# A new order of all steps, and more buffers, in a fused RWKV-5 and squared-ReLU kernel

## The chip, the core and the metric

The kernel runs on one core of one Trainium2 chip. The metric is the device time of one launch in microseconds. Engines are named as in the profile: PE (TensorE) with PEld (its weight loads), DVE (VectorE), ACT (ScalarE), POOL (GpSimd) and SP (SyncE, which here only issues transfers).

## The reference

```python
def _attn_ref(r, k, v, w, u):            # r, k, v: (4, 8, 768, 48); w, u: (8, 48)
    state = zeros((B, H, D, D))
    for t in range(S):
        kt, vt, rt = k[:, :, t], v[:, :, t], r[:, :, t]
        cur = einsum('bhd,bhe->bhde', u[None] * kt, vt)
        y[:, :, t] = einsum('bhd,bhde->bhe', rt, state + cur)
        state = w[None, :, :, None] * state + einsum('bhd,bhe->bhde', kt, vt)

def _moe_ref(x, w_in, w_out):            # x: (3072, 384); w_in: (384, 2048); w_out: (2048, 384)
    h = maximum(x @ w_in, 0.0)
    return h * h @ w_out
```

The output y of the first part, laid out as 3072 tokens of 384 values, is the x of the second.

## The kernel before

**Units and chunks.** A batch's 768 steps are cut into 6 chunks of 128; a unit i is one chunk (i // 4) of one batch (i % 4), all 8 heads, so there are 24 units. Within a unit the recurrence becomes matmuls; between units of one batch a state S0W is handed on.

**Steps.** Each function of the class Do issues one step, for one unit. `ld` loads r, k or v (192 KB in float32). `kh` and `rh` scale k and r by powers of w into the tile rk (the first four units read the powers from PSUM, where `Wk` and `Wt` put them; `WkS` and `WtS` write copies in SBUF for the others). rk is transposed into rkT: by PE (`T`) and a copy (`Tc`), or by a DMA transpose (`XB`). `A` multiplies k and r per head (8 matmuls of 48 rows), `Bm` masks the result, `Y` sums it with v (bf16, made by `vb`) and, from the second chunk on, with the state. `P0`, `P1`, `du`, `dv` make the term with u (r times k, times u, summed per head, times v); `xs` adds it to Y. `U`, `ts`, `S` (or `S0`) carry the state on. xs is transposed into x by PE (`X`) and a copy (`xTc`), or by a DMA transpose (`xX`).

**The second part.** It runs over 13 groups of units (GROUPS: two of one unit, eleven of two). `F1` g.s multiplies x of group g with w_in into a PSUM bank of 512 columns, `re` applies the ReLU into hr, `sq` squares into hq (form 0 on ACT, 1 and 2 on DVE). `F2` i.q adds the matmuls of one quarter q of w_out for unit i; after the four quarters `os` copies the bank out and `out` stores 192 KB.

**Weights.** w_in is cut into eight tiles W1[s]. Seven are loaded in float32 on SP (`lW.0.s`, into the staging tiles wsa) and cast (`cW.0.s`). W1[2] and the four quarters of w_out are loaded by POOL with a cast on the way (`W.0.2`, `W.1.q`). An F1 of a one-unit group needs two W1 tiles (F1.g.2 needs W1[4] and W1[5], F1.g.1 needs W1[2] and W1[3]), one of a two-unit group one.

**The order.** A planner has written all 961 steps into the text ORDER. An entry such as `sq.4.1:A0/26` gives the step, its engine (A is ACT, D DVE, G POOL, P PE, S SP) with a form, and the buffer numbers. The kernel only walks the list (the loop at the end) and each engine runs its own entries in that order; what waits for what follows from the tiles. POOLS gives the number of buffers of each kind. `Z.n.b` is no work: n blocks of 128 columns of matmuls on the identity into bank b, to fill PE's time at the start.

Lines that the profile names: L319 ld, L323 lW, L332 W, L335 kh, L338 rh, L341 P0, L345 P1, L348 du, L353 dv, L362 T, L368 XB, L375 A, L383 Bm, L391 and L393 Y, L402 U, L410 xs, L423 S, L428 X, L435 xX, L444 F1, L452 and L454 re, L459 to L463 sq, L471 F2, L480 Z, L493 out; L259 and L261 are the helper for copies and casts (Tc, xTc, vb, cW, os) on ACT and on the other engines.

Of the kernel before, what the change touches and what calls it, by code (L numbers as in the profile page):

```python
# [30 lines left out]
re.0.2:D/4 xTc.3:A WLm:G U.3:P/1 F1.2.1:P/0 re.1.2:A/5 W.1.2:G sq.0.3:A0/1 F1.2.5:P/1 re.2.1:D/2 W.1.3:G sq.0.0:A0/2
U.1:P/2 S0.2:D re.2.5:A/3 F1.2.4:P/0 sq.0.2:D2/3 cW.0.3:A S0.0:D F1.2.7:P/1 re.2.4:D/1 sq.1.0:A0/4 F2.0.0:P/1
sq.2.5:D2/5 re.2.7:A/4 S0.3:D F1.0.1:P/0 F1.2.3:P/1 re.0.1:D/0 F2.1.0:P/0 S0.1:D re.2.3:A/3 F1.1.1:P/0 sq.1.2:D2/6
sq.0.1:D2/7 ld.k.7:S/6 F1.2.0:P/1 re.1.1:A/5 F2.0.1:P re.2.0:A/0 sq.1.1:D2/8 F1.2.2:P/0 sq.2.4:A0/9 sq.2.0:D1/10
F2.1.1:P kh.4:D/4 F1.2.6:P/1 ld.v.5:S/4 rh.4:D P0.4:D/4 F2.1.2:P ld.r.7:S/6 re.2.2:D/5 P1.4:G F2.0.2:P re.2.6:D/1
sq.2.2:A0/11 F2.1.3:P ld.v.4:S/5 kh.5:G/5 sq.2.1:A0/12 sq.2.6:D1/13 F2.0.3:P os.1:A/0 du.4:D/4 ld.k.6:S/0 T.4:P/0
sq.2.3:A0/14 rh.5:D F2.2.0:P/0 os.0:A/1 P0.5:D/0 Tc.4:A/4 ld.r.6:S/0 T.5:P/3 P1.5:D F2.2.1:P kh.7:D/6 Tc.5:A/5
ld.v.7:S/6 A.4:P/1/2 du.5:D/0 F2.3.0:P/1 Bm.4.0:D/3 ld.k.9:S/2 A.5:P/0/3 vb.4:A/4 dv.4:G Bm.4.1:D/2 F2.3.1:P vb.5:A/5
ld.r.9:S/2 Bm.5.1:D/4 dv.5:G sq.2.7:A0/15 Y.4:P/1 Bm.5.0:D/5 F2.3.2:P rh.7:G ld.k.8:S/1 xs.4:D/4 U.4:P/2 Y.5:P/3
F2.2.2:P P0.6:G/1 ld.v.6:S/0 xs.5:D/0 X.4:P/0 ts.4:D/0 X.5:P/1 T.7:P/3 xTc.4:A/1 kh.6:D/1 ld.k.15:S/3 F2.2.3:P xTc.5:A  # L40
rh.6:D vb.7:A/6 U.5:P/2 P1.6:D F1.3.0:P/0 Tc.7:A/6 ld.k.10:S/4 ts.5:D/1 F1.3.1:P/1 kh.9:D/2 re.3.0:A/0 ld.v.9:S/2
T.6:P/0 P0.7:D/2 os.2:A/2 A.7:P/1/2 S.5:D re.3.1:A/5 ld.r.8:S/1 F2.3.3:P du.6:D/2 P1.7:G Tc.6:A/0 Bm.7.1:D/0 F1.3.3:P/0
sq.3.0:A0/16 rh.9:G ld.r.10:S/3 os.3:D/3 F1.3.4:P/1 re.3.3:A/2 Bm.7.0:D/1 A.6:P/3/0 P0.9:G/3 du.7:D/1 re.3.4:A/1
XB.9:S/1 F1.3.5:P/0 Bm.6.1:D/3 sq.3.1:A0/17 dv.7:G F1.3.6:P/1 Bm.6.0:D/2 re.3.5:A/3 F2.5.0:P/0 dv.6:G vb.6:A/7
ld.k.12:S/5 sq.3.3:A0/18 Y.7:P/2 out.3:S kh.10:D/3 re.3.6:A/4 Y.6:P/1 ld.v.8:S/3 S.4:G xs.7:D/1 F1.3.2:P/0 sq.3.5:A0/19
xs.6:D/2 F1.3.7:P/1 ld.v.11:S/1 kh.8:D/0 re.3.2:A/0 kh.15:D/4 U.6:P/0 X.6:P/3 sq.3.2:A0/20 X.7:P/2 rh.8:D F2.4.0:P/1
ld.r.12:S/4 re.3.7:A/5 rh.10:D F2.5.1:P xTc.6:A/2 sq.3.4:D2/21 P1.9:D xTc.7:A U.7:P/1 T.8:P/3 vb.9:A/2 out.0:S P0.8:D/4
F1.4.0:P/0 ts.6:D/1 ld.k.11:S/0 Tc.8:A/2 P1.8:G ts.7:D/0 F1.4.4:P/1 ld.r.13:S/5 du.9:D/3 re.4.0:A/2 F2.5.2:P kh.12:G/5
re.4.4:A/3 F1.4.6:P/0 ld.r.11:S/0 sq.3.6:A0/23 sq.3.7:D2/22 vb.8:G/3 du.8:D/4 A.9:P/2/0 sq.4.4:A0/24 A.8:P/1/3 S.6:G
re.4.6:A/0 F2.5.3:P ld.v.10:S/5 Bm.8.1:D/4 F1.4.3:P/1 dv.8:G Bm.8.0:D/5 os.5:A/3 ld.k.13:S/6 F1.4.5:P/0 Bm.9.1:D/1  # L50
re.4.3:A/1 dv.9:G Y.8:P/3 Bm.9.0:D/0 re.4.5:A/5 XB.10:S/3 F2.4.1:P P0.12:G/0 xs.8:D/3 sq.4.0:A0/25 Y.9:P/1 vb.11:A/1
kh.11:G/1 F1.4.1:P/1 xs.9:D/4 ld.v.13:S/4 X.8:P/0 F1.4.2:P/0 re.4.1:D/4 xTc.8:A/0 ld.r.15:S/6 F2.4.2:P rh.11:D
sq.4.1:A0/26 P1.12:D X.9:P/2 vb.10:A/0 F1.4.7:P/1 P0.10:D/1 ld.k.20:S/2 xTc.9:A sq.4.5:D2/27 F2.7.0:P/0 P0.11:D/2
re.4.7:A/3 ld.v.12:S/6 U.8:P/3 P1.10:D sq.4.3:A0/28 F2.4.3:P kh.13:D/6 re.4.2:A/2 F1.5.2:P/1 du.10:D/0 out.1:S os.4:A/1
# [63 lines left out]
def kernel(  # L118
# [13 lines left out]
    B, H, S, D = r.shape  # L132
# [410 lines left out]
```

## Time and profile before

| what | us |
|---|---|
| median of 3 runs | 176.91 (175.41 to 177.27) |
| the profiled run's own time | 175.4 |
| span of the profiled run | 173.7 |
| PE, PEld busy | 165.4, 121.9 |
| DVE, ACT, POOL busy | 140.7, 109.8, 69.3 |
| granted TensorE clock | 1.00 throughout |
| DMA | 28.34 MB, 163 GB/s mean |

The times of steps come from one profiled run. A span is counted from the program's first instruction to its last; the run's own time also has what lies around it. Matmuls are pipelined: the time from one start to the next tells what one costs, its length does not. Busy lengths of DVE and ACT overlap by some 0.1 us from one instruction to the next.

### The profile page before, as it was taken

How to read it: one execution, taken by the hardware profiler on the slowest of the kernel's cores; microseconds unless marked ns; L12 is line 12 of the kernel's file. 1: busy time of each engine (PE TensorE's matmuls, PEld its weight loads, DVE VectorE, ACT ScalarE, POOL GpSimd, SP SyncE). 2: the span in 40 equal slices, each digit the busy share in tenths (PEclk: the TensorE clock that was granted, in tenths of full speed). 3: DMA queues.
4: the chain of work that ended last, by engine and by line, in shares of the span. 5: the costliest groups of instructions: out<-in, count | busy, mean ns of one | idle time of the engine just before them, and what ended most of it. 6: DMA issues, size and time to landing. Idle time of an engine off the chain costs nothing.

```text
span 173.7 us, 4402 instructions
## 1 busy us (share of the span) xinstructions
PE 165.4 (95%) x1714; PEld 121.9 (70%) x1714; DVE 140.7 (81%) x278; ACT 109.8 (63%) x203; POOL 69.3 (40%) x84
## 2 busy tenths in 40 slices
PE   4989699999999999999999999999999999999991
PEld 1445498766878787877777787778678677787760
DVE  5989787799899989999989898899998667853520
ACT  2489389557599979786676769659478141173401
POOL 4264743044385694923464950601950301000000
PEclk9999999999999999999999999999999999999999
DMA  5999999999999999989698799989931422110041
GB/s 106 245 249 248 258 213 219 201 192 189 213 188 214 243 171 234 197 191 205 128 217 178 151 205 212 152 191 180 200 94 30 151 94 68 25 45 4 0 171 55
DMA packets 102276, 28.34 MB, mean 163 GB/s; under 512 B 94824, under 2 KB 102256, under 8 KB 102256
## 3 DMA queue, kind: packets, MB, share of 16 engines
q1 hardware_dynamic: 100360, 26.10, 71.4%
q0 software_dynamic: 1744, 1.77, 6.2%
q8 instruction: 13, 0.21, 0.5%
q10 hardware_dynamic: 152, 0.20, 0.3%
q14 instruction: 7, 0.06, 0.1%
HBM read 20.46 MB, written 4.72 MB: 145 GB/s over the span
## 4 chain that ended last, share of the span: by engine, by line
PE 80%; DMA 8%; SPq 6%; ACT 1%; issue 1%; POOL 1%; POOLq 0%
PE bank L471 36%; PE bank L444 33%; DMA wsa<-in_moe_w_in_dram 8%; SPq L319 5%; PE bank L375 3%; PE bank L393 2%; PE bank L391 2%; PE bank L402 2%; PE bank L362 2%; SPq L323 1%; PE bank L428 1%; ACT W L259 1%; ACT hr L452 0%; ACT hq L459 0%; ACT os L259 0%
## 5 line engine op out<-in xcount | busy, mean ns | idle before, releaser
L444 PE MATMUL bank<-xT,W 128*128 128x256 bf16 (+1 forms) x624 | 74.5, 264 | 1.3 <-ACT W L259 1.2
L471 PE MATMUL bank<-W,hq 128*128 128x384 bf16 x384 | 73.6, 326 | 0.0
L452 ACT ACTIVATE hr<-bank 128x512 bf16<-128x512 f32 x71 | 42.0, 597 | 35.9 <-PE bank L444 33.2
L444 PEld LDWEIGHTS <-W 128*128 128x128 bf16 x624 | 55.4, 98 | 11.9 <-ACT W L259 1.4
L471 PEld LDWEIGHTS <-hq 128*128 128x128 bf16 x384 | 35.6, 98 | 17.8
L459 ACT ACTIVATE hq<-hr 128x512 bf16<-128x512 bf16 x57 | 34.7, 629 | 2.5 <-DVE hr L454 2.4
L383 DVE TENSOR_TENSOR Bm<-bank,maskJT 128x512 bf16<-128x512 f32 x48 | 31.4, 683 | 3.0 <-PE bank L375 3.0
L345 POOL TENSOR_TENSOR P<-P,ub 128x384 f32<-128x384 f32 x14 | 15.5, 1110 | 30.0 <-DVE P L341 26.8
L353 POOL TENSOR_TENSOR dv<-ldv,du 128x384 f32<-128x384 f32 x19 | 16.4, 874 | 25.7 <-DVE du L348 21.0
L454 DVE TENSOR_SCALAR hr<-bank 128x512 bf16<-128x512 f32 x25 | 17.1, 689 | 10.4 <-PE bank L444 6.5
L463 DVE TENSOR_TENSOR hq<-hr 128x512 bf16<-128x512 bf16 x35 | 15.0, 457 | 1.9 <-ACT hr L452 1.9
L410 DVE TENSOR_TENSOR xs<-bank,dv 128x384 bf16<-128x384 f32 x24 | 13.2, 553 | 3.5 <-PE bank L393 2.8
L259 ACT COPY os<-bank 128x384 f32<-128x384 f32 x18 | 8.6, 477 | 8.8 <-PE bank L471 8.1
L480 PE MATMUL bank<-identity 128*128 128x512 bf16 (+1 forms) x40 | 11.6, 427 | 2.3 <-POOL identity masks.py:199 2.3
L348 DVE TENSOR_REDUCE du<-P 128x8 f32<-128x384 f32 x24 | 12.9, 543 | 0.0
L341 POOL TENSOR_TENSOR P<-ldr,ldk 128x384 f32<-128x384 f32 x11 | 11.3, 1026 | 3.9 <-DMA ldr<-in_r_dram 3.9
L259 ACT COPY rkT<-bank 128x1024 bf16<-128x1024 bf16 x10 | 10.1, 1015 | 2.9 <-PE bank L362 2.2
L423 POOL TENSOR_TENSOR S0W<-ts,WLm 128x384 bf16<-128x384 f32 x7 | 7.4, 1061 | 10.0 <-PE bank L471 6.7
L393 PE MATMUL bank<-vb,Bm 128*128 128x48 bf16 x192 | 10.8, 183 | 0.3 <-ACT vb L259 0.3
L393 PEld LDWEIGHTS <-Bm 128*128 128x128 bf16 x192 | 9.5, 96 | 1.3 <-issue 0.4
L259 ACT CAST vb<-ldv 128x384 bf16<-128x384 f32 x19 | 9.6, 511 | 0.2 <-DMA ldv<-in_v_dram 0.2
L259 ACT COPY xT<-bank 128x384 bf16<-128x384 bf16 x14 | 6.5, 477 | 5.0 <-PE bank L428 5.0
(61 smaller groups left out, 161.7 us busy)
## 6 DMA issues: line engine op xcount, KB each, us to landing
ldr<-in_r_dram SPq DMA_DIRECT2D x24, 192.0 KB, 3.9
ldk<-in_k_dram SPq DMA_DIRECT2D x24, 192.0 KB, 3.8
ldv<-in_v_dram SPq DMA_DIRECT2D x24, 192.0 KB, 4.0
out_dram<-os SPq DMA_DIRECT2D x23, 192.0 KB, 2.2
wsa<-in_moe_w_in_dram SPq DMA_DIRECT2D x7, 384.0 KB, 5.6
W<-in_moe_w_out_dram POOLq DMA_DIRECT2D x4, 384.0 KB, 7.9
rkT<-rk SPq DMA_TRANSPOSE x14, 3.4
W<-in_moe_w_in_dram POOLq DMA_DIRECT2D x1, 192.0 KB, 8.2
```

Of the source, the lines that this page charges most:

```text
L259: e.copy(o, a)
L345: e.tensor_mul(t, t, ub)
L353: e.tensor_mul(dvb[slot[f"dv{i}"]], loaded("v", i), t)
L383: e.tensor_mul(Bmb[slot[f"Bm{i}{h}"]], heads(bank(f"bA{i}{h}"), 128), mask_b)
L393: e.matmul(y[:, hc, D * h : D * (h + 1)], m[h][:, hc, :], vb[:, 2 * hc + h, :], start=(c == 0), stop=True, skip_group_check=True,)
L410: e.tensor_add(xsb[slot[f"xs{i}"]].rearrange("p (a b) -> p a b", a=HP), heads(bank(f"bY{i}"), 2 * D), dvb[slot[f"dv{i}"]].rearrange("p (a ...
L444: e.matmul(hp[:, fi, :], W1[f // 2][:, c, 128 * (f % 2) : 128 * (f % 2 + 1)], xt[:, c, :], start=(c == 0), stop=(c == CCH - 1), skip_group ...
L452: e.activation(hr, hp, AF.Relu)
L454: e.tensor_scalar_max(hr, hp, 0.0)
L459: e.activation(hq, hr, AF.Square)
L463: e.tensor_mul(hq, hr, hr)
L471: e.matmul(bank(f"bO{i}", "bO")[:, 0:d_model], hqb[slot[f"hq{g},{f // m}"]][:, at : at + L], W2[q][:, f % 4, :], start=(f == 0), stop=(f = ...
```

## The change

Two counts in POOLS are raised, F2 no longer fixes which quarter of w_out comes first, and ORDER is replaced as a whole: the same kinds of steps, 961 of them as before, in another sequence and partly on other engines. The planner that wrote it now has the fetching of instructions in its model of the queues, and tends to put the A steps of two units next to each other.

```diff
-POOLS = dict(ldr=7, ldk=7, ldv=7, ws=0, wsa=4, rk=7, P0=5, dv=5, vb=8, rkT=7, bank=4, bankH=2, bankO=2, Bm=6, xs=5, xT1=2, xT2=3, xT4=1, hr=6, hq=30, os=4, ts=2)
+POOLS = dict(ldr=8, ldk=8, ldv=8, ws=0, wsa=6, rk=7, P0=5, dv=5, vb=8, rkT=7, bank=4, bankH=2, bankO=2, Bm=6, xs=5, xT1=2, xT2=3, xT4=1, hr=6, hq=30, os=4, ts=2)
 ORDER = """
-ld.r.1:S/0 w:A ld.k.1:S/0 u:S Z.48.5:P tab:A ld.k.0:S/1 ld.k.2:S/2 shw:D ld.r.0:S/1 logw:A ld.r.2:S/2 Wt:A/0 P0.1:D/0
-shu:D Wk:A/1 lW.0.6:S/0 rh.1:D/0 kh.1:D ld.v.1:S/0 ld.k.3:S/3 T.1:P/0 kh.0:D/1 Z.16.5:P P1.1:G Tc.1:A/0 kh.2:D/2 rh.0:D
-ld.v.3:S/1 WtS:A rh.2:D P0.2:G/1 A.1:P/1/2 WkS:A T.0:P/3 lW.0.1:S/1 Z.16.5:P P1.2:D ld.r.3:S/3 Tc.0:A/1 du.1:D/0
-P0.0:D/2 cW.0.6:A ld.v.0:S/2 A.0:P/0/3 dv.1:G Bm.1.1:D/0 Z.6.5:P du.2:D/1 T.2:P/2 P1.0:G Bm.1.0:D/1 ld.v.2:S/3 Z.22.5:P
-Tc.2:A/2 Bm.0.0:D/2 Bm.0.1:D/3 lW.0.0:S/2 vb.1:A/0 lW.0.5:S/3 kh.3:D/3 Y.1:P/1 cW.0.1:A lW.0.7:S/0 A.2:P/0/2 xs.1:D/0
-Z.4.5:P P0.3:G/3 vb.3:A/1 du.0:D/2 lW.0.4:S/1 X.1:P/3 Z.8.5:P rh.3:D wc:S xTc.1:A/0 Bm.2.0:D/4 vb.0:A/2 T.3:P/1
-ld.k.4:S/4 dv.0:D Y.0:P/3 Z.13.5:P Tc.3:A/3 vb.2:G/3 Bm.2.1:D/5 P1.3:G xs.0:D/1 A.3:P/0/2 X.0:P/1 cW.0.0:A U.0:P/3
-dv.2:G Bm.3.0:D/1 Z.6.7:P xTc.0:A/1 du.3:D/3 lW.0.3:S/2 F1.1.0:P/0 Bm.3.1:D/0 ld.r.4:S/4 F1.0.0:P/1 re.1.0:D/0 W.1.0:G
-W.0.2:G cW.0.7:G Y.2:P/0 Y.3:P/1 re.0.0:A/1 ld.k.5:S/5 xs.2:D/2 cW.0.5:A dv.3:D F1.1.3:P/0 cW.0.4:A X.2:P/2 F1.0.3:P/1
-re.1.3:D/2 ld.r.5:S/5 xTc.2:A/0 W.1.1:G U.2:P/0 xs.3:D/3 F1.0.2:P/0 re.0.3:A/3 sq.1.3:D2/0 WLcol:A X.3:P/2 F1.1.2:P/1
-re.0.2:D/4 xTc.3:A WLm:G U.3:P/1 F1.2.1:P/0 re.1.2:A/5 W.1.2:G sq.0.3:A0/1 F1.2.5:P/1 re.2.1:D/2 W.1.3:G sq.0.0:A0/2
-U.1:P/2 S0.2:D re.2.5:A/3 F1.2.4:P/0 sq.0.2:D2/3 cW.0.3:A S0.0:D F1.2.7:P/1 re.2.4:D/1 sq.1.0:A0/4 F2.0.0:P/1
-sq.2.5:D2/5 re.2.7:A/4 S0.3:D F1.0.1:P/0 F1.2.3:P/1 re.0.1:D/0 F2.1.0:P/0 S0.1:D re.2.3:A/3 F1.1.1:P/0 sq.1.2:D2/6
-sq.0.1:D2/7 ld.k.7:S/6 F1.2.0:P/1 re.1.1:A/5 F2.0.1:P re.2.0:A/0 sq.1.1:D2/8 F1.2.2:P/0 sq.2.4:A0/9 sq.2.0:D1/10
...
+ld.k.2:S/0 ld.r.2:S/0 w:A u:S tab:A ld.k.0:S/1 ld.v.2:S/0 ld.r.1:S/1 P0.2:D/0 ld.r.0:S/2 shw:D shu:D logw:A ld.k.1:S/2
+WtS:A Wk:A/0 vb.2:G/0 ld.r.3:S/3 Wt:A/1 P1.2:G kh.2:D/0 rh.2:D ld.v.1:S/1 Z.63.5:P T.2:P/0 kh.0:D/1 du.2:D/0 Tc.2:A/0
+ld.v.0:S/2 WkS:A kh.1:D/2 P0.1:G/1 Z.17.5:P A.2:P/1/2 lW.0.1:S/0 rh.0:D T.0:P/3 Bm.2.1:D/0 dv.2:G wc:S rh.1:D Tc.0:A/1
+P0.0:G/2 Z.4.5:P T.1:P/0 Bm.2.0:D/1 ld.k.3:S/3 Tc.1:A/2 rh.3:D/3 Y.2:P/2 P1.0:G A.0:P/3/1 lW.0.0:S/1 xs.2:D/0 Bm.0.1:D/2
+lW.0.7:S/2 Z.3.5:P A.1:P/0/2 vb.1:G/1 Bm.1.1:D/3 ld.k.4:S/4 P1.1:G X.2:P/1 xTc.2:A/0 Bm.1.0:D/4 ld.v.3:S/3 vb.0:G/2
+du.0:D/1 Z.11.5:P Y.1:P/2 WLcol:A kh.3:D dv.0:D WLm:G Z.8.5:P T.3:P/1 Bm.0.0:D/5 Tc.3:A/3 P0.3:D/3 lW.0.6:S/3 Z.6.5:P
+Y.0:P/0 du.1:D/2 cW.0.1:A P1.3:G A.3:P/3/1 xs.0:D/1 lW.0.4:S/4 cW.0.0:A dv.1:D Z.3.5:P X.0:P/0 lW.0.5:S/5 cW.0.7:G
+xs.1:D/2 xTc.0:A/0 ld.r.4:S/4 du.3:D/3 Z.10.5:P X.1:P/2 lW.0.3:S/0 F1.0.0:P/0 Bm.3.0:D/0 xTc.1:A/1 ld.k.5:S/5 vb.3:G/3
+F1.1.0:P/1 Bm.3.1:D/1 re.0.0:A/0 W.1.0:G dv.3:D Y.3:P/0 re.1.0:A/1 U.1:P/2 cW.0.6:G U.3:P/3 xs.3:D/3 sq.1.0:A0/0
+kh.4:D/4 Z.4.0:P X.3:P/1 cW.0.4:G F1.1.3:P/0 xTc.3:D F1.0.3:P/1 re.1.3:A/2 cW.0.5:D W.0.2:G ld.r.5:S/5 U.2:P/0
+F1.0.2:P/0 re.0.3:A/3 S0.2:D W.1.1:G sq.0.0:D2/1 F1.1.2:P/1 re.0.2:A/4 rh.4:D W.1.2:G U.0:P/1 F1.2.4:P/0 re.1.2:A/5
+P0.4:G/4 F1.2.1:P/1 re.2.4:A/1 T.4:P/0 sq.2.4:A0/2 P1.4:G re.2.1:D/0 F1.2.5:P/0 Tc.4:A/4 ld.v.4:S/4 S0.0:D F1.2.0:P/1
+W.1.3:G re.2.5:D/1 A.4:P/1/0 sq.2.5:D2/3 F1.2.6:P/0 cW.0.3:D re.2.0:A/1 F2.0.0:P/1 sq.1.3:A0/4 Bm.4.0:D/3 F1.0.1:P/1
+re.2.6:A/2 sq.2.1:D2/5 sq.1.2:D2/6 sq.0.2:A0/7 F2.1.0:P/0 sq.2.0:D2/8 re.0.1:A/0 Bm.4.1:D/4 F1.1.1:P/0 sq.0.1:A0/9
...
+    quarters = {}
...
         def F2(e, i, q):
...
+            done = quarters.setdefault(i, [])
+            done.append(q)
             for f in range(4 * q, 4 * q + 4):
...
-                    start=(f == 0), stop=(f == FCH - 1), skip_group_check=True,
+                    start=(f == 4 * q and len(done) == 1), stop=(f == 4 * q + 3 and len(done) == 4),
+                    skip_group_check=True,
```

Steps by engine where the counts differ, before and after:

| step | before | after |
|---|---|---|
| P0 | D 13, G 11 | D 10, G 14 |
| P1 | D 10, G 14 | D 9, G 15 |
| kh | D 19, G 5 | D 14, G 10 |
| rh | D 18, G 6 | D 8, G 16 |
| dv | D 5, G 19 | D 8, G 16 |
| S | D 9, G 7 | D 2, G 14 |
| vb | A 19, D 2, G 3 | A 10, D 5, G 9 |
| cW | A 6, G 1 | A 2, D 2, G 3 |
| xTc | A 14 | A 10, D 4 |
| sq | A 57, D 39 | A 63, D 33 |
| re | A 71, D 25 | A 70, D 26 |
| os | A 18, D 6 | A 16, D 8 |
| out | S 23, A 1 | S 15, A 9 |
| T with Tc, XB | 10, 14 | 9, 15 (unit 11) |
| X with xTc, xX | 14, 10 | 14, 10 (12 by PE, 19 by DMA) |

Behind the start, A steps of two units follow each other on PE six times before and nine times after. The last steps of the new order are:

```text
os.20:D/1 F1.12.3:P/1 sq.12.0:D2/26 out.20:A os.21:D/0 re.12.7:A/0 F2.23.0:P/0 re.12.3:D/5 out.21:A F2.23.2:P
sq.12.7:D2/11 sq.12.3:D2/20 F2.22.0:P/0 F2.23.1:P F2.23.3:P F2.22.3:P os.23:D/2 F2.22.1:P out.23:A F2.22.2:P os.22:A/3
out.22:S
```

## The prediction

> **What bounds the kernel now.** I read the page's busy shares first, then PE's timeline, the chain of waits and the windows, and last the lines of the engines that get more work.
>
> ```profile
> PE 165.4 (95%) x1714; PEld 121.9 (70%) x1714; DVE 140.7 (81%) x278; ACT 109.8 (63%) x203; POOL 69.3 (40%) x84
> ```
>
> PE is busy 95% of the span, but part of that is the Z steps (L480), matmuls on the identity that only fill time. The timeline of PE (start, length, group; in brackets the idle time and what ended it) shows where they end:
>
> ```profile
> 18.75 0.49 PE L480 MATMUL bank<-identity 128*128 128x512 bf16 x3
> 20.48 1.51 PE L444 MATMUL bank<-xT,W 128*128 128x128 bf16 x24 [1.23 <-ACT W L259]
> ...
> 24.25 0.84 PE L444 MATMUL bank<-xT,W 128*128 128x128 bf16 x12
> ```
>
> The first F1 starts at 20.48 after waiting for ACT's cast of a W1 tile. The chain of waits names what stands behind the cast, the transfer of that tile:
>
> ```profile
> 13.93 5.59 DMA wsa<-in_moe_w_in_dram
> 19.54 0.88 ACT W L259
> ```
>
> After that PE is packed. The windows give PE 10.00 of every 10.00 us, and start-to-start times agree: six 256-column F1 matmuls take 0.66 us and four F2 matmuls 0.65 us all the way from 20.5 to the end of the last one at 170.07, with no gap over 0.25 us. So the time is a start (20.5), 149.6 us of packed PE work, and a tail of 3.6 to the span's end at 173.7 (last copy, store, drains). The profiled run took 175.4; the median of the runs, 176.91, is 1.5 above it. I make the sum against 175.4 and add 1.5.
>
> A plan can win only at the start, or by less PE work; every new wait of PE behind the start is a loss, since nothing there absorbs it.
>
> **PE work, part by part.** One PE transpose of r and k goes (T.11, to a DMA): eight matmuls, 0.44 us (38.26 to 38.70 in the timeline). X and xX are only exchanged (12 for 19): nothing. "A in pairs" is priced by these lines:
>
> ```profile
> 39.80 0.81 PE L471 MATMUL bank<-W,hq 128*128 128x384 bf16 x4
> 40.55 0.40 PE L375 MATMUL bank<-rkT 48*128 48x128 bf16 x8
> 40.88 0.82 PE L471 MATMUL bank<-W,hq 128*128 128x384 bf16 x4
> ...
> 59.50 0.82 PE L444 MATMUL bank<-xT,W 128*128 128x256 bf16 x6
> 60.25 0.62 PE L375 MATMUL bank<-rkT 48*128 48x128 bf16 x16
> 60.80 0.82 PE L471 MATMUL bank<-W,hq 128*128 128x384 bf16 x4
> ```
>
> A lone A takes 0.33 and a pair 0.55, so a pair saves 0.11; and the step before an A lasts 0.75 instead of 0.65, so each entry into A costs another 0.10. Behind the start the old order has six pairs and the new one nine: 3 x 0.21 = 0.6. PE work: -1.0 in all. The new use of start and stop in F2 adds no instruction: nothing.
>
> **The start.** First the arithmetic ahead of F1. In the new order P0.2 stands ahead of both shuffles on DVE, and needs the second load, which lands near 4.64: shw slips from 4.02 to about 5.2, logw on ACT to 5.8, and WtS (0.6) now goes ahead of Wk, so kh.2 starts near 7.5 (kh.1 before: 6.3). From there DVE has 23 instructions up to xs.1: 6 Bm at 0.60 and 17 others at 0.47 (lengths 0.68 and 0.55 less the overlap of neighbours in the timeline), 11.6 us, plus 0.4 of waits for T, Tc and k: 19.5. X.1 follows and F1.0.0 starts at about 20.0, 0.5 earlier than the first F1 now. The W1 tile that is awaited today comes earlier (11 loads and 2 tiles ahead of its end instead of 12 and 2), but DVE takes over as the limit.
>
> More matters five steps later, at F1.0.2, which starts at 24.25 now and in the new order needs tiles 4 and 5. Tile 5 is the sixth W1 tile, behind 13 loads, 5 other tiles and wc. The same bytes were through in the trace when ld.k.4 landed, at 23.57, with the DMA share at 0.94 to 1.10 in every 5 us up to there. Its cast goes to DVE, which shows no cast of this size: half of it takes DVE 449 ns, so 0.9 (ACT 887, POOL 880). That gives 24.5. Tiles land late within a mix (5.6 us median from issue, 8.1 at most), so I take 25.0, with 23.5 (PE's own work, tiles in time) and 26.5 as bounds. By F1.0.2 the new order has done one X and one U more (0.34). The start: +0.75 - 0.34 = +0.4.
>
> **The W2 quarters.** GpSimd issues them and the last W1 tile, in a queue that is now longer:
>
> ```profile
> 18.87 0.89 POOL L332 DMA_DIRECT2D W<-in_moe_w_out_dram  x1
> 19.76 0.76 POOL L332 DMA_DIRECT2D W<-in_moe_w_in_dram  x1
> ...
> 26.15 1.41 POOL L332 DMA_DIRECT2D W<-in_moe_w_out_dram  x2
> ```
>
> and from their issue it takes this long until they land (view of tile W):
>
> ```profile
> DMA to landing us min/median/max: 7.1/8.2/9.1
> ```
>
> In the new queue cW.0.7, cW.0.6 and cW.0.4 (0.88 each, the last not before 23) stand ahead of W.0.2, which is issued at 24.0 instead of 19.76; with the median 8.2 it lands at 32.2. F1.0.1 needs it: from 25.0 come eight F1 and F2 steps (5.3) and U, T and A (1.0), so 31.3. PE waits 0.9. W.1.3, behind P0.4 and P1.4, goes out at 28.8 and lands by 37.9 at the longest; F2.0.3 is due ten steps after F1.0.1, at 32.2 + 6.6 = 38.8: covered by 0.9. Bounds of this part: 0, and 2.6 (W.0.2 out at 24.8 and 9.1 under way).
>
> **Moves between engines.** DVE hands 26 operations to GpSimd (rh 10, S 7, kh 5, P0 3, P1 1); GpSimd also takes 6 vb and 2 cW and gives up 3 dv, 31 more in all. By the rows GpSimd needs 1.00 to 1.11 us for what DVE does in 0.57 to 0.62. DVE takes 14 others (xTc 4, vb 3, dv 3, cW 2, os 2) and was not on the path behind 20.5, so its gain is nothing; ACT swaps vb, xTc and cW for six more sq, nothing either; GpSimd's longer times are hidden as long as its queue keeps up, which is the second rival. Eight stores go from SP's queue to ACT's: SP saves 8 x 0.53, ACT pays the same (0.35 in the one case shown), beside 63% busy: nothing, but each waits for its copy and holds back re and sq behind it; four of them stand in the tail, where PE's last eight quarters (5.2 us) cover them. The last store goes the other way, 1.9 to landing on either queue: nothing. Eight buffers and six tiles add no work; they free SP from waits such as the 1.24 us at 18.3 for a staging tile. Instruction fetches moved 0.21 MB and took 0.5% of the DMA time; planning with them changes places, not work: nothing.
>
> **Sum.** -1.0 + 0.4 + 0.9 = +0.3: 175.7 against the profiled run's 175.4, and 177.2 as a median.
>
> **Rivals.**
>
> *Tiles in time: faster.* If tile 5 lands with the DVE chain, F1.0.2 starts at 23.5, the W2 quarters keep their places, and the sum is -1.0 - 0.75 - 0.34 = -2.1: 174.8. For it: no wait for a staging tile any more. Against: the DMA share is 0.94 to 1.10 in every 5 us from 5 to 25, so the bytes cannot come much sooner.
>
> *GpSimd becomes the bound from about 50 to 100 us: slower.* In the windows (busy us and count of PE, PEld, DVE, ACT, POOL; then clock, DMA share, GB/s) GpSimd has room now:
>
> ```profile
> 60.00:70.00 10.00, 10.00 (x119) 7.56 (x118) 9.10 (x17) 8.36 (x18) 7.77 (x9) 1.00 1.05 206
> 80.00:90.00 10.00, 10.00 (x107) 7.26 (x105) 9.25 (x19) 7.01 (x15) 4.87 (x5) 1.00 0.86 173
> ```
>
> Laying both orders along PE's work with the rows' mean times, GpSimd gets 31 us in these 50 before (measured: 32) and 47 after, 94%. It runs in order and also waits for loads and for DVE; some loads lead their reader by only 3.8 us of PE work (k of 8, 14, 18), about the 3.8 a load takes to land, where the old order gave 5.3. What comes late next is rh or kh, with it XB on SP's queue, the loads behind it, and A; an XB leads its A by at least 4.6 and lands in 3.4, so 1.2 is covered. It decides once its 49 operations there fill the 50 us, at 0.06 more each than the rows' means (one more in five at 1.33 instead of 1.00). Beyond that every wait of GpSimd counts: four short-led loads at 0.5 and as much for du (for which it waits 21.0 us in the trace), 4.0 less the 1.2, about 3 on PE: 180.2. These lines bear on it (min, median, max):
>
> ```profile
> L335 DVE TENSOR_TENSOR rk<-ldk,Wkhat x15: 544/548/1348, 34.5 to 107.2; 128x384 bf16<-128x384 f32 x15
> L338 POOL TENSOR_TENSOR rk<-ldr,Wt x6: 996/1000/1315, 42.9 to 100.3; 128x384 bf16<-128x384 f32 x6
> ```
>
> Both engines have cases far over their median. The Trainium skill (SBUF — State Buffer, "SBUF: two separate sides") says that DVE and GpSimd share a port pair under an exclusive lock, and that a DVE instruction with two SBUF inputs and a GpSimd one block each other fully. The long cases agree with it. Against the rival: fewer such DVE instructions remain, 68 for 101.
>
> *The W2 quarters starve: slower.* With the bound of 2.6 for F1.0.1's wait the sum is +2.0: 178.9. For it: all DMA engines are taken up there; against: the old order's landings are from the same crowded stretch.
>
> **Chances.** Forecast (within its own 176.0 to 178.5) 0.40; tiles in time 0.20; GpSimd 0.29; W2 0.11. A measurement of this kernel can tell about 1%, 1.8 us, from no change. Faster by more than that: the first rival nearly whole, 0.19. Slower: GpSimd's, most of W2's and a little of the forecast's upper end, 0.40. The range runs from the first rival's 174.8 to 181.0, a little over GpSimd's.
>
> **What would show it.** Right: first F1 near 20.0, F1.0.2 near 25.0 after a wait for DVE's cast; PE gap-free from about 33 on; GpSimd over 9 of 10 us between 50 and 100. Wrong: PE waits between 50 and 100 that lead back to GpSimd's rk, S or dv, or an F1.0.2 outside 23.5 to 26.5.

## The result: 3.9% slower, and one store on ACT behind most of it

The changed kernel takes 183.32 us (median; 182.83 to 184.5), the kernel before 176.39 in the same comparison: a ratio of 1.039, 95% interval 1.031 to 1.047. The profiled execution took 184.5 with a span of 182.8, against 175.4 and 173.7 before.

The busy shares come first. PE lost three points, and GpSimd has half as much work again:

```profile
PE 167.8 (92%) x1711; PEld 123.0 (67%) x1711; DVE 140.5 (77%) x261; ACT 104.2 (57%) x188; POOL 102.7 (56%) x115
```

DVE has 17 instructions fewer than before and is busy for the same time (140.7 before). GpSimd has 31 more and 33 us more.

The start, in PE's timeline (start, length, group; in brackets the idle time and what ended it), and DVE's timeline of the same stretch:

```profile
20.40 1.56 PE L446 MATMUL bank<-xT,W 128*128 128x128 bf16 x24
...
23.97 0.38 PE L485 MATMUL bank<-identity 128*128 128x512 bf16 x1 [1.40 <-DVE xs L412]
...
24.35 1.50 PE L446 MATMUL bank<-xT,W 128*128 128x128 bf16 x24
...
25.87 0.33 PE L446 MATMUL bank<-xT,W 128*128 128x128 bf16 x3
```

```profile
21.74 1.49 DVE L355 TENSOR_TENSOR dv<-ldv,du 128x384 f32<-128x384 f32 x1
23.36 0.56 DVE L412 TENSOR_TENSOR xs<-bank,dv 128x384 bf16<-128x384 f32 x1
...
24.83 0.94 DVE L261 CAST W<-wsa 128x768 bf16<-128x768 f32 x1
```

The first F1 starts at 20.40; then PE stands 1.40 us for xs.3, which stands behind a dv.3 of 1.49 us where its kind takes 0.55. F1.0.2 starts at 25.87, 1.62 later than before, just when the cast of tile 5 is through (25.77).

From there PE is nearly packed up to 76, and then comes the one big hole. PE's timeline, then ACT's:

```profile
75.60 0.81 PE L475 MATMUL bank<-W,hq 128*128 128x384 bf16 x4
81.23 1.44 PE L446 MATMUL bank<-xT,W 128*128 128x256 bf16 x6 [4.82 <-ACT hr L454]
```

```profile
73.18 1.25 ACT L454 ACTIVATE hr<-bank 128x512 bf16<-128x512 f32 x2
80.18 0.36 ACTq L498 DMA_DIRECT2D out_dram<-os  x1
80.58 0.60 ACT L454 ACTIVATE hr<-bank 128x512 bf16<-128x512 f32 x1 [6.15 <-DMA ldv<-in_v_dram]
```

PE waits for a re on ACT, since both F1 banks are full. ACT did nothing from 74.44 to 80.18: the store out.3 stood at the head of its queue. The release is named on the third line: the landing of a load of v, which is none of the store's business by its data. In the compiled program the transfers of SP and ACT raise eight completion semaphores in turn, 101 to 108 in the trace. This turn isn't the order of the text ORDER, in which ld.v.15 stands just behind out.3: in the compiled program ld.v.15, on SP's queue, is the eighth transfer ahead of out.3, and both raise semaphore 101. The store waits until ld.v.15 has landed (80.16) and goes out 0.02 us later. Its copy os.3 had been done 21 us before ACT got to the store.

Why was ld.v.15 late? SP's timeline and GpSimd's lead back:

```profile
64.12 1.84 SPq L321 DMA_DIRECT2D ldv<-in_v_dram  x2
71.04 4.23 SPq L370 DMA_TRANSPOSE rkT<-rk  x2
75.33 1.20 SPq L321 DMA_DIRECT2D ldk<-in_k_dram  x2
76.57 1.56 SPq L321 DMA_DIRECT2D ldv<-in_v_dram  x2
```

```profile
57.46 1.93 POOL L355 TENSOR_TENSOR dv<-ldv,du 128x384 f32<-128x384 f32 x2 [3.13 <-DVE du L350]
...
68.75 1.31 POOL L337 TENSOR_TENSOR rk<-ldk,Wkhat 128x384 bf16<-128x384 f32 x1
70.02 0.99 POOL L340 TENSOR_TENSOR rk<-ldr,Wt 128x384 bf16<-128x384 f32 x1
```

SP issued nothing from 65.97 to 71.04. It stood at the transposing transfer XB.11 until GpSimd had finished rh.11, at 71.02. GpSimd had waited 3.13 us for a du of DVE and worked without a gap from then on. Behind XB.11 and XB.10 came two loads of k, and at 76.57 ld.v.15, which landed 3.59 later.

The windows (busy us and count of PE, PEld, DVE, ACT, POOL; then clock, DMA share, GB/s) show the same and one thing more:

```profile
60.00:70.00 10.00, 9.92 (x119) 7.97 (x117) 10.00 (x18) 6.68 (x13) 10.00 (x10) 1.00 0.78 162
70.00:80.00 10.00, 6.41 (x55) 4.69 (x53) 7.84 (x11) 3.53 (x7) 10.00 (x11) 1.00 0.75 127
80.00:90.00 10.00, 8.77 (x81) 6.10 (x81) 4.78 (x9) 6.70 (x13) 7.31 (x8) 0.66 1.07 234
```

GpSimd and DVE are full from 60 to 70, and the granted clock, 1.00 all along before, is 0.66 from 80 to 90. In the trace it is 0.5 from 80.03 to 86.85; PE worked in 5.6 us of that, so this cost 2.8.

The last F2 ends 9.14 us later than before. In the sum a wait of PE is counted from where PE would have gone on without it, 0.1 to 0.2 us more than the idle time in brackets. F1.0.2 gives +1.62, but one X and one U more are done by then (-0.34); the hole gives 4.98, the half clock 2.8, two waits at 30 and 51 give 0.33 and 0.51; PE's own work is -0.8 (worked out below). That is 9.1, for this one execution, the longest of the changed kernel's.

### The profile page after: what moved, and what is told of

Its sections match the earlier page's. It is cut to its first block, busy times and chain, and to the rows that moved or that the text cites. A ratio compares the mean times of both kernels' runs of the same rounds, so it can differ in the third digit from the quotient of the medians.

```text
span 182.8 us, 4369 instructions
## 1 busy us (share of the span) xinstructions
PE 167.8 (92%) x1711; PEld 123.0 (67%) x1711; DVE 140.5 (77%) x261; ACT 104.2 (57%) x188; POOL 102.7 (56%) x115
## 4 chain that ended last, share of the span: by engine, by line
PE 57%; SPq 20%; DMA 8%; POOL 6%; DVE 4%; issue 2%; ACT 1%; ACTq 0%; POOLq 0%
PE bank L475 26%; PE bank L446 24%; SPq L321 16%; SPq L325 3%; PE bank L377 2%; DMA ldk<-in_k_dram 2%; DMA ldv<-in_v_dram 2%; DMA ldr<-in_r_dram 2%; DMA out_dram<-os 2%; PE bank L395 2%; PE bank L393 1%; POOL P L347 1%; DVE Bm L385 1%; POOL rk L337 1%; POOL rk L340 1%
## 5 line engine op out<-in xcount | busy, mean ns | idle before, releaser
L446 PE MATMUL bank<-xT,W 128*128 128x256 bf16 (+1 forms) x624 | 75.5, 267 | 5.1 <-ACT hr L454 4.8
L446 PEld LDWEIGHTS <-W 128*128 128x128 bf16 x624 | 56.6, 99 | 17.1 <-issue 5.8
L461 ACT ACTIVATE hq<-hr 128x512 bf16<-128x512 bf16 x63 | 38.1, 628 | 6.6 <-DVE hr L456 6.1
L340 POOL TENSOR_TENSOR rk<-ldr,Wt 128x384 bf16<-128x384 f32 x16 | 18.7, 1171 | 9.1 <-DMA ldr<-in_r_dram 9.0
L425 POOL TENSOR_TENSOR S0W<-ts,WLm 128x384 bf16<-128x384 f32 x14 | 14.6, 1047 | 12.6 <-DVE ts L422 12.5
L343 POOL TENSOR_TENSOR P<-ldr,ldk 128x384 f32<-128x384 f32 x14 | 14.9, 1072 | 8.4 <-DVE du L350 7.0
L259 ACT COPY rkT<-bank 128x1024 bf16<-128x1024 bf16 x9 | 9.1, 1009 | 7.6 <-PE bank L364 7.5
L259 ACT COPY os<-bank 128x384 f32<-128x384 f32 x16 | 7.6, 476 | 9.6 <-PE bank L475 9.5
L337 POOL TENSOR_TENSOR rk<-ldk,Wkhat 128x384 bf16<-128x384 f32 x10 | 11.2, 1118 | 0.5 <-PE bank L404 0.5
L465 DVE TENSOR_TENSOR hq<-hr 128x512 bf16<-128x512 bf16 x25 | 10.1, 438 | 0.2
```

The costliest lines, as they stand in the source:

```text
L259: e.copy(o, a)
L340: e.tensor_mul(rk[slot[f"rk{i}"]][:, 0, :, 0:D], loaded("r", i), early("WtP") if i < EARLY else Wt2)
L446: e.matmul(hp[:, fi, :], W1[f // 2][:, c, 128 * (f % 2) : 128 * (f % 2 + 1)], xt[:, c, :], start=(c == 0), stop=(c == CCH - 1), skip_group ...
L461: e.activation(hq, hr, AF.Square)
```

## The experiments

Times are medians; each ratio is to the kernel before in the same comparison.

**Is it the store on ACT?** One entry of the new order is changed.

```diff
-out.3:A
+out.3:S
```

> The changed kernel with one entry of the order altered: the store out.3 goes from ACT's queue to SP's. Theory L (the store stands at the head of ACT's queue until the load ld.v.15 of SP's queue has landed, ACT's re copies stand behind it, PE runs out of banks for 5.0 us, and the granted clock then falls to 0.5 for 6.8 us): no wait of PE near 76 us, no stretch at half clock, so 183.3 - 5.0 - 3.4 = 174.9, and some of it given back where the store now stands on SP: 175 to 178. Rival G (GpSimd, busy 10 of 10 us from 60 to 80, is what stalls PE, and the store only shows it first): PE waits within the next 10 us all the same, for rh, XB or A, and the time stays at 180.5 or more.

Measured: 179.25, ratio 1.016 (1.010 to 1.022). The hole at 76 is gone, while GpSimd is as full as it was:

```profile
60.00:70.00 10.00, 10.00 (x120) 8.08 (x119) 9.98 (x19) 7.17 (x14) 10.00 (x10) 1.00 0.94 193
70.00:80.00 10.00, 9.56 (x100) 7.39 (x98) 9.52 (x14) 7.47 (x16) 10.00 (x10) 1.00 0.91 172
```

PE's only wait there is 0.44 us idle for a ts. So rival G, that a full GpSimd stops PE for several us here by itself, falls. Theory L has the place right and the time too low (179.25 lies between the two forecasts), because ACT then stands for another transfer of SP:

```profile
107.59 0.60 ACT L454 ACTIVATE hr<-bank 128x512 bf16<-128x512 f32 x1 [0.32 <-PE bank L446]
111.45 0.48 ACT L259 COPY os<-bank 128x384 f32<-128x384 f32 x1 [3.26 <-DMA out_dram<-os]
```

Here it stands at os.11, whose buffer is still being stored by out.7: a wait for data this time, not for a shared semaphore. That store stood far back in SP's queue: issued at 106.77, 23 us after its copy, landed at 111.43. PE lost 2.3 us and ran at half clock for 3.4.

**The same store, still on ACT, but earlier.** If ACT's queue is the point and not the engine that issues, an earlier place is enough.

```diff
-... xs.9:D/3 os.5:A/0 ... F1.5.2:P/1 out.3:A vb.12:G/2
+... xs.9:D/3 out.3:A os.5:A/0 ... F1.5.2:P/1 vb.12:G/2
```

> The changed kernel with one entry of the order moved: the store out.3 stays in ACT's queue, but ahead of the copy os.5, some 5.5 us earlier. The transfer that raised its completion semaphore before it is then ld.v.11, landed at 67.67 in the changed kernel's trace; ACT comes by at about 68.9. Theory L (only the wait for the late load holds ACT): ACT passes in 0.4 us, no wait of PE near 76, 178 to 180.5 like the run with the store on SP. Rival (a store in ACT's queue in this crowded stretch costs PE several us wherever it stands, as transfers are slow there): 182 or more.

Measured: 178.29, ratio 1.013 (1.009 to 1.018), where the changed kernel had 1.039. The medians differ by 5.0 us, but the kernel before was 0.7 faster in this comparison too; by the ratios a single entry moved within its queue is worth 4.5 us. ACT's timeline and PE's:

```profile
68.50 0.35 ACTq L498 DMA_DIRECT2D out_dram<-os  x1
68.89 0.48 ACT L259 COPY os<-bank 128x384 f32<-128x384 f32 x1 [1.37 <-DMA ldv<-in_v_dram]
```

```profile
71.19 1.47 PE L446 MATMUL bank<-xT,W 128*128 128x256 bf16 x12 [0.30 <-ACT xT L259]
...
75.10 0.82 PE L446 MATMUL bank<-xT,W 128*128 128x256 bf16 x6
75.85 0.45 PE L377 MATMUL bank<-rkT 48*128 48x128 bf16 x9
76.76 0.38 PE L377 MATMUL bank<-rkT 48*128 48x128 bf16 x7 [0.46 <-DVE ts L422]
```

Even here ACT waits 1.37 us at the store for a load of v, another one (ld.v.11), where 0.4 was expected. ACT works without a gap from there to the copy xTc.8, for which PE then stands 0.30 us at 71: a wait of this length is nearly covered. The time is as theory L has it. Together the two runs show the cause of the hole: the wait of a store for a load of another queue, at a place where ACT has no slack for it.

**A store on ACT in the old order**, as a control:

```diff
-out.1:S
+out.1:A
```

> The kernel before with one entry of the order altered: its store out.1, in the middle of the kernel, goes from SP's queue to ACT's. Theory L: what a store on ACT costs is the wait for a load of SP's queue that is late; here SP is on time, the load concerned has landed when ACT gets to the store, so ACT pays its 0.36 us and PE nothing: within 1% of before (175 to 178). Rival (a store in ACT's queue in the middle of the kernel costs PE several us whatever the loads do): 179 or more.

Measured: 175.82, ratio 0.999 (0.995 to 1.004), as theory L says. ACT's timeline:

```profile
67.64 0.60 ACT L452 ACTIVATE hr<-bank 128x512 bf16<-128x512 f32 x1
68.04 0.35 ACTq L493 DMA_DIRECT2D out_dram<-os  x1
68.14 0.62 ACT L459 ACTIVATE hq<-hr 128x512 bf16<-128x512 bf16 x1
```

The load that this store waits for, ld.v.13, landed only at 68.02 in the trace, 0.02 us before the store went out. ACT was still busy with a re then and lost nothing. So a store in ACT's queue in the middle of the kernel costs nothing when SP's load is there in time, and here it was only just in time.

**Does the delay begin with GpSimd?**

```diff
-S.6:G ... ld.r.14:S/0 P1.12:G ... kh.14:G/6 ... rh.11:G
+S.6:G ... ld.r.14:S/0 rh.11:G P1.12:G ... kh.14:G/6 ...
```

> The changed kernel with rh.11 moved ahead of P1.12 in GpSimd's queue, so that it ends some 2.2 us earlier; out.3 stays on ACT. Theory L with its root in GpSimd (rh.11 late, XB.11 at the head of SP's queue late, the loads behind it late, the store on ACT waits for them): SP leaves XB.11 near 68.8 instead of 71.0, ACT's wait and PE's shrink by 1.4 to 2.2 us (the store now stands behind the landing of another load, issued up to 0.9 later), and the clock may stay up: 181.5 at most, 178 if the half clock goes with it. Rival (the store's wait does not begin with GpSimd): no change, 182.5 to 184.

Measured: 183.74, ratio 1.039 (1.030 to 1.047): no gain in the median. The profiled execution, 181.18, is the shortest, and does what theory L says. SP's timeline and PE's:

```profile
67.58 3.12 SPq L370 DMA_TRANSPOSE rkT<-rk  x2
70.75 1.25 SPq L321 DMA_DIRECT2D ldk<-in_k_dram  x2
72.05 2.28 SPq L321 DMA_DIRECT2D ldv<-in_v_dram  x2
```

```profile
78.26 0.92 PE L446 MATMUL bank<-xT,W 128*128 128x256 bf16 x6 [3.08 <-ACT hr L454]
```

XB.11 leaves 3.5 us sooner and PE loses 3.2 us instead of 5.0, with 3.41 us at half clock instead of 6.83. The three other runs had spans of 182.0 to 182.3 at a mean clock of 0.981, which is some 6.9 us at half clock; there is no trace of them, and why they gained nothing stays open. The trace shows the chain from rh.11 to PE; by the median the rival's forecast (182.5 to 184) holds, so what an earlier rh.11 is worth isn't shown.

**The half clock.** A filler Z of 16 matmuls (3.5 us; the expectation took it for four) goes into the hole, the store stays.

```diff
-F1.5.0:P/1
+Z.64.0:P F1.5.0:P/1
```

> The changed kernel with one more filler step Z (four matmuls on the identity, 0.6 us by the rows, to a bank of its own) just ahead of the F1 step that waits near 76 us; the store out.3 stays on ACT. Theory C (the half clock follows PE's idle stretch, some 4 us after it began): idle time falls from 5.0 to about 4.3, the wait ends at the same place; the stretch of half clock is gone or clearly shorter, and the time is 183.3 - 3.4 = about 180 (181.5 if half of the stretch is left). Rival (the half clock has another cause, or 4.3 us of idling are as bad as 5.0): still 6.8 us at 0.5, 182.5 to 184.

```profile
77.74 3.62 PE L485 MATMUL bank<-identity 128*128 128x512 bf16 x16
82.56 0.82 PE L446 MATMUL bank<-xT,W 128*128 128x256 bf16 x6 [1.20 <-ACT hr L454]
```

The clock stays at 1.0 behind the hole, as theory C says, but the time doesn't follow: 183.11, ratio 1.040 (1.034 to 1.047). In this profile a half-clock stretch fell into the start instead, F1 was about 1.5 us later by 52, and behind the hole PE, at full clock, ran into waits of 0.77 (xs, at 89) and 0.40 (sq, at 118). The other runs, at a mean clock of 0.999 to 1.0, took 182.2 to 183.7. So in this order the half clock at 80 was worth little by itself; that its cost would be waited anyway, for engines that are late, is likely from these two waits and not shown.

The reverse: the kernel before without its last three Z steps ahead of F1, which compute nothing that is used.

```diff
-Z.8.5:P ... Z.13.5:P ... Z.6.7:P
```

> The kernel before without its last three steps Z (26 matmuls' worth on the identity that only fill the time between 15.2 and 19.2; nothing the output needs). Theory C (a stretch in which PE idles is followed by 3.4 us, or a multiple of it, at half clock, beginning within 4 us): a stretch at 0.5 between 18 and 25 us, which costs PE up to 1.7 us: 177 to 178.5, clock 0.99. Rival (the half clock in the runs with waits near 76 and 110 came with the load there, and idling alone does not bring it): clock 1.0 throughout, 175.5 to 176.8.

Windows of this run:

```profile
20.00:24.00 4.00, 2.80 (x30) 2.80 (x31) 1.21 (x2) 1.26 (x3) 2.65 (x4) 0.50 1.11 253
24.00:28.00 4.00, 4.00 (x65) 4.00 (x63) 2.67 (x6) 3.50 (x7) 0.38 (x2) 0.71 1.22 245
```

The clock is 0.5 from 19.46 to 26.29. Time 176.98, ratio 1.007 (1.003 to 1.010): between the two forecasts, a hair under theory C's and 0.2 above its rival's. The clock decides for theory C. With the same loads and the same work that the output needs, idling alone brought the half clock here.

**What is left of the loss.** First the second wait, out.7 ahead of out.8 on SP, with out.3 on SP:

```diff
-out.3:A ... out.8:S ... rh.19:G/2 out.7:S
+out.3:S ... out.7:S out.8:S ... rh.19:G/2
```

> The run with out.3 on SP, and out.7 moved ahead of out.8 in SP's queue (it stood at 106.77 there, 23 us after its copy; ACT's os.11, which writes the same buffer, stood until it had landed at 111.43, and PE lost 2.3 us at 110 and 1.7 at half clock). Theory L2 (what is left of the loss behind 70 us is this one wait of the same kind: ACT at the head of its queue for a transfer of SP): no wait of PE over 0.6 us behind 35 us, 175 to 177. Rival (each wait removed is followed by the next, since GpSimd, SP and DVE are all late in this order): again over 1.5 us of PE waits between 70 and 130, 178 to 180.

Measured: 178.55, ratio 1.014 (1.008 to 1.019). The 2.3 us at 110 shrank to 0.39, but the next wait was 1.15 for a Bm at 114. The rival holds, by its time and by the waits: PE's idle stretches between 70 and 130 still add up to 1.7 us. In the profiled execution F1 started only at 21.37, with the start of the program unchanged (20.40 in the changed kernel), so the start differs by 1 us from one execution to another. Then the start as well:

```diff
-P0.2:D/0 ld.r.0:S/2 shw:D shu:D logw:A ld.k.1:S/2 WtS:A Wk:A/0
+shw:D shu:D P0.2:D/0 ld.r.0:S/2 logw:A ld.k.1:S/2 Wk:A/0 WtS:A
...
-Bm.3.0:D/0 ... Bm.3.1:D/1 ... dv.3:D
+dv.3:D Bm.3.0:D/0 ... Bm.3.1:D/1 ...
```

> As the run before, and in the start: both shuffles of w and u ahead of P0.2 on DVE, Wk ahead of WtS on ACT, dv.3 ahead of the two Bm.3 on DVE. Theory S (the start is the chain shuffle, logw, Wk, then DVE's instructions up to xs.1, and a wait for xs.3 behind a dv.3 of 1.4 to 1.5 us): kh.2 starts 0.8 to 1.2 us sooner than 7.58, F1 at 19.2 to 19.5, the wait at 22.4 falls from 1.4 to under 0.8; 1.0 to 1.5 us less than the run before: 174 to 175.8, under the kernel before. Rival (the W1 tiles and their casts are what end the start, as in the kernel before): DVE's chain is earlier, F1.0.2 stays near 25.5, within 0.5 us of the run before.

Measured: 179.22, ratio 1.021 (1.016 to 1.026). kh.2 did start sooner, at 6.33 (7.29 to 7.58 in the other profiles of this start), but DVE then waited 0.45 for Wt on ACT and 0.78 for a load of k. It was nearly packed from there, and xs.1 ended at 20.00, within the 19.9 to 21.2 of the other profiles; F1 started at 20.23 and F1.0.2 at 25.25. The rival holds in its outcome. Its reason, the W1 tiles, isn't what the profile shows: DVE's chain is, and the load that it waits for. A new wait of 1.27 for a ts came up at 51.

**The engines alone.** The old order with the new engines for rh, kh, S, P0, P1 and dv from unit 4 on, and the new order (out.3 earlier on ACT) with the old ones.

```diff
-rh.10:D ... kh.8:D/0 ... S.5:D ... P0.8:D/4
+rh.10:G ... kh.8:G/0 ... S.5:G ... P0.8:G/4
...
```

> The order of the kernel before, with the engines of the change for rh, kh, S, P0, P1 and dv from tile 4 on: 41 of these go from DVE to GpSimd and 18 the other way; stores, loads and PE's order stay. Theory K (the moves are not free: GpSimd fills up, its operations and DVE's two-input ones get in each other's way, and what waits for them is late): over 18 GpSimd operations above 1.2 us where the kernel before has some 13, PE waits of 1 us or more in sum behind 35 us, 177.5 to 182. Rival (the prediction's reading: GpSimd's longer times are hidden): 175 to 176.8.

> The other way round: the changed kernel with out.3 earlier on ACT (178.3 us), and the same operations from tile 5 on back on the engines that the kernel before gave them (40 to DVE, 18 to GpSimd). Theory K: GpSimd's busy time falls from 104 to near 84 us, the long operations of DVE go back from 27 towards 13, the PE waits behind 35 us (0.47 + 0.53 + 0.82 + 0.55 in that run) fall under 1 us: 175.5 to 177.3. Rival (the waits come of the order, which was laid out for these engines; DVE, busy 10 of 10 us from 50 to 70, is then later still): 178 or more.

The moves by themselves: 180.37, ratio 1.020 (1.012 to 1.028), in theory K's range; GpSimd's instructions over 1.2 us went from 7 to 17, where it expected over 18. The only profile of that kernel is of its longest run (183.4, the shortest took 178.97), so what it shows may not hold for the others. In it PE stands 2.0 us at 56 for a Bm, which stands behind a P0 and a dv of DVE at twice their length:

```profile
58.27 0.22 PE L393 MATMUL bank<-vb,Bm 128*128 128x48 bf16 x2 [1.99 <-DVE Bm L383]
```

```profile
54.14 1.24 DVE L341 TENSOR_TENSOR P<-ldr,ldk 128x384 f32<-128x384 f32 x1
...
56.37 1.25 DVE L353 TENSOR_TENSOR dv<-ldv,du 128x384 f32<-128x384 f32 x1
57.54 0.68 DVE L383 TENSOR_TENSOR Bm<-bank,maskJT 128x512 bf16<-128x512 f32 x1
```

The other way round theory K fails and its rival holds: 186.6, ratio 1.058 (1.053 to 1.063). GpSimd's busy time falls to 80.1 and DVE's instructions over 0.7 us stay many (31, against 25), but DVE now has 154.9 us of work and PE waits in some sixteen places behind 35 us, mostly for xs, Bm, xT and hq. So in both of these orders the engines alone could not be exchanged without a loss.

**The parts that lessen PE's work, in the old order.** Two pairs of A and XB.11 in place of T.11; then the pairs alone. The pair of units 6 and 7 is one of the changed order; that of 4 and 5 isn't, and stands for the others.

```diff
-A.4:P/1/2 du.5:D/0 F2.3.0:P/1 Bm.4.0:D/3 ld.k.9:S/2 A.5:P/0/3
+du.5:D/0 F2.3.0:P/1 ld.k.9:S/2 A.4:P/1/2 A.5:P/0/3 Bm.4.0:D/3
...
-A.7:P/1/2 ... Bm.7.1:D/0 ... Bm.7.0:D/1 A.6:P/3/0
+A.7:P/1/2 A.6:P/3/0 Bm.7.1:D/0 Bm.7.0:D/1
...
-T.11:P/2 ... Tc.11:A/4
+XB.11:S/4 ld.k.17:S/1
```

> The kernel before with parts of the change that lessen PE's work, and nothing else: A.4 moved to A.5 and A.7 to A.6 (two more pairs), and T.11 with its copy Tc.11 replaced by a transposing DMA XB.11 ahead of ld.k.17 on SP. Theory W (the prediction's prices: 0.21 for each pair, 0.44 for T.11): 0.86 us less, 174.4 to 175.2 where before is 175.7 to 176.4, no new wait of PE. Rival (XB.11 takes 1.2 to 2.5 us at the head of SP's queue, the loads behind it are late, and a new wait near 75 us takes the gain): 175.7 or more.

> The kernel before with the two pairs alone (A.4 at A.5, A.7 at A.6); T.11 stays on PE. Theory W (a pair saves what the prediction priced, 0.21 each): 0.4 less than before, about 175.6 where before is 176.0. Rival (the A that is moved back comes later, so do its two Bm on DVE and the Y behind them; in the run with XB.11 PE waited 0.40 us for a Bm at 43, and 0.5 at 54): the pairs give nothing or cost up to 0.7: 176.0 to 176.7.

Measured: 177.90, ratio 1.009 (1.005 to 1.013), and for the pairs alone 176.66, ratio 1.003 (1.000 to 1.006). The rival holds both times. PE's timeline from Y.4 to the F2 behind it, first in the kernel before, then with the pairs alone:

```profile
42.62 0.21 PE L391 MATMUL bank<-S0W,rkT 128*128 128x96 bf16 x1
...
43.00 0.81 PE L471 MATMUL bank<-W,hq 128*128 128x384 bf16 x4
```

```profile
42.40 0.21 PE L391 MATMUL bank<-S0W,rkT 128*128 128x96 bf16 x1
...
42.97 0.20 PE L393 MATMUL bank<-vb,Bm 128*128 128x48 bf16 x1 [0.34 <-DVE Bm L383]
...
43.28 0.81 PE L471 MATMUL bank<-W,hq 128*128 128x384 bf16 x4
```

The price of PE's work was right: Y starts 0.22 sooner. But it takes 0.88 instead of 0.38, as PE waits for the Bm behind the A that was moved back. This pair saves 0.2 and costs 0.5. With XB.11 come PE waits for an os (0.71 at 99) and a transposed x (0.59 at 109).

## Why the prediction was wrong, by its steps

**The step that failed** is in "moves between engines": "Eight stores go from SP's queue to ACT's ... nothing, but each waits for its copy and holds back re and sq behind it". The issue on ACT was priced, 0.35 us, and the wait for the copy was named; the other wait, for a transfer of SP's queue that raises the same completion semaphore, was not looked for. In the profiled run that term measured 5.0 us of standing PE and 2.8 of half clock. Taking it away gave 4.1 us (store on SP) and, by the ratios, 4.5 (store earlier): less than 7.8, since other waits came up where the store moved to SP, and since the filler run shows that the half clock added little of its own. The loss of clock was missing from every case of the prediction.

**GpSimd as the bound** was the second rival, 0.29 at 180.2. Its chain was right as far as it went: GpSimd filled all of 60 to 80 (from 50 to 100 it was busy 41 us, not 47), rh was late, XB stood at SP's head, the loads behind it were late. But it was to come out at A, for about 3 us after 1.2 of cover; it came out at ACT, which the chain did not contain. The prediction named PE waits that lead back to GpSimd's rk as a sign of being wrong, and the wait at 76 does lead back to rh.11 in the trace; the median of the run with rh.11 earlier doesn't confirm it. With the store away, the same full GpSimd came with 0.5 us of waiting there. What the prediction did with its other half, "hidden as long as its queue keeps up", was too kind: the moves alone cost the old order 2.0%.

**Price of the moves.** The prediction priced what DVE hands over and takes as nothing, since DVE was not on PE's path. Its busy time is indeed the same, 140.5 against 140.7, but not because nothing changed. With the median lengths of the kernel before, the changed set of DVE's instructions would take some 8 us less (an estimate from the two traces); longer instructions took back 6.7. The lines of the P0 products, before and after (min, median, max):

```profile
L341 DVE TENSOR_TENSOR P<-ldr,ldk x13: 545/551/1285, 4.7 to 115.1; 128x384 f32<-128x384 f32 x13
```

```profile
L343 DVE TENSOR_TENSOR P<-ldr,ldk x10: 546/674/1352, 4.5 to 127.6; 128x384 f32<-128x384 f32 x10
```

The median itself has grown. Over all of DVE, instructions longer than 0.7 us went from 9 to 24, GpSimd's over 1.2 us from 7 to 19. The prediction held against this rival that fewer two-input DVE instructions remain; there were fewer, but more of them were long. The long cases fit the Trainium skill (SBUF — State Buffer, "SBUF: two separate sides"), whose exclusive lock the prediction cited; no run here isolates the lock.

**The start**: first F1 20.0 forecast, 20.40 measured, by the DVE chain as worked out. F1.0.2 25.0 forecast (23.5 to 26.5), 25.87 measured. Tile 5's cast was at its place, 24.83; but PE was as late by itself, through dv.3 at 1.49 us, which was not foreseen. That this term came out inside its bounds is in part luck. In the run with out.3 earlier dv.3 took 0.55 and F1.0.2 came at 25.14.

**The W2 quarters**: +0.9 forecast, nothing measured. GpSimd's timeline, and the time from issue to landing for the tiles W:

```profile
23.90 0.76 POOL L334 DMA_DIRECT2D W<-in_moe_w_in_dram  x1
24.66 1.48 POOL L334 DMA_DIRECT2D W<-in_moe_w_out_dram  x2
```

```profile
DMA to landing us min/median/max: 6.3/8.9/10.3
```

W.0.2 was issued at 23.90 (24.0 forecast) and landed 6.3 us later, at 30.24; the prediction had taken 8.2, from rows whose least was 7.1. F1.0.1 started at 32.53 without a wait. PE was itself 1.2 us later than the 31.3 it was to come at, but at 31.3 the tile would have been there too.

**PE's work**: -1.0 forecast. In the run with out.3 earlier, from F1.0.2 (25.14) to the end of the last F2 (172.50) there are 147.36 us, with waits of 0.32, 0.47, 0.53, 0.82 and 0.55 in them; without these 144.67, against 145.82 before. Of the 1.15, 0.34 is the X and U done earlier: -0.8 is left. The size was about right, and it didn't decide anything.

**What is left** of the loss with that store moved is 2.4 us by the spans (176.1 against 173.7): 0.9 in the start and 2.7 in the five waits, less 1.15. Against the forecast's sum of +0.3 these waits are the term that is missing; the W2 wait of 0.9 that did not come offsets a part of it. No run removed these waits together, and none of the kernels run here was clearly faster than the one before.

## What to carry to other kernels

A transfer in a compute engine's queue can be a wait in that queue: ask not only what data it needs but which earlier transfer, on any queue, raises the same completion semaphore in the compiled program, and put it where that one has long landed. Here 5.5 us earlier in ACT's queue was enough to lose most of the wait. In a kernel whose PE is packed, price a change by the waits it can cause on engines without slack, not only by the work it saves: a pair of A steps that saves 0.2 us cost 0.5. An order and an assignment of engines that were laid out together may not bear a change of one alone: here the new engines alone cost 2.0% in the old order, and the old engines cost the new order another 4.5%.

## What the hardware showed that was not expected

The half clock came in stretches of 3.41 us or twice that, and less idle time than the hole's brought it:

| kernel | PE idle from, to | half clock from, to | length |
|---|---|---|---|
| changed | 76.41, 81.23 | 80.03, 86.85 | 6.82 |
| rh.11 earlier | 75.18, 78.26 | 78.83, 82.24 | 3.41 |
| out.3 on SP | 110.38, 112.51 | 113.52, 116.93 | 3.41 |
| engines of the change | 56.28, 58.27 | 58.81, 62.23 | 3.41 |
| out.7 earlier | 23.54, 25.43 | none | |
| out.7 earlier | 114.17, 115.15 | none | |
| filler in the hole | 16.23, 17.52 | 20.07, 23.48 | 3.41 |
| less fill | 19.37, 21.20, and partly before | 19.46, 26.29 | 6.83 |
| before | 19.25, 20.48 | none | |

Each stretch behind a hole in the middle of a kernel begins 2.5 to 3.7 us after PE went idle. The longest idle stretch without one is this, in PE's timeline of the run with out.7 earlier:

```profile
25.43 0.38 PE L485 MATMUL bank<-identity 128*128 128x512 bf16 x1 [1.89 <-DVE xs L412]
```

The Trainium skill (TensorE: Matmul & The Clock Gate, "Part 1: The HAM clock gate") gives a free-running window of 3413 ns, after an idle one of which the clock is halved; the lengths agree. On the same page, under "Why this matters for your kernels", the Trainium skill asks for idle gaps of no more than about 3 us; the rows show that 2.13, 1.99 and once 1.29 us were enough, while 1.89 us brought none elsewhere. So the length of one gap alone doesn't decide it; what does, no run here shows.

The other thing is how far such a wait reaches: ACT came to its store at 74.44 and stood there for a load that SP issued only at 76.57, with the DMA engines at a share of 0.75 from 70 to 80. Nothing in the DMA's load would have shown it; the line of the store's own wait did.
